# Convolving the third and fourth block of a fused conv and MLP kernel together, in bf16 quarter tiles

## The chip, the cores and the metric

The kernel runs on one core of one Trainium2 chip. The metric is the device time in microseconds (us) of one execution, as the median of several runs. The engines are TensorE (PE in the profile, with PEld for its weight loads), VectorE (DVE), ScalarE (ACT), GpSimd (POOL) and SyncE (SP, which here only starts transfers).

## The reference, cut to what matters

```python
# x: (8, 4096, 192), weight: (8, 7)
w = softmax(weight, axis=-1)                       # 8 heads, 7 taps
out[b, s, h, g] = sum_k w[h, k] * x_pad[b, s + k, h, g]    # causal depthwise conv, 24 channels a head
h = out.reshape(32768, 192) @ moe_w_in             # 192 -> 2048
g = h * sigmoid(beta * h)
y = g @ moe_w_out                                  # 2048 -> 192, float32
```

## The kernel before

The 32768 tokens are two streams `s` of 16384 tokens, which are worked on side by side. The 192 channels are cut in three groups `kk` of 64, so that 64 partitions hold one group; w_in's 2048 columns are 16 chunks `fc` of 128. The token axis is cut in steps (line 66): steps 0 and 1 have 128 tokens of each stream, step 2 has 256, steps 3 to 6 have 256 (line 68), steps 7 to 10 have 384, and the rest 512. A "block" is 128 tokens of both streams; step 0 is the first block, step 1 the second, step 2 the third and fourth. Everything here is in program order, written out by hand (`pin`).

A step has three parts. The convolution gives `xc` (bf16). The first matmul (mm1) multiplies by w_in into PSUM (`ph`), and ScalarE's Silu activation brings it to SBUF as `g`. The second matmul (mm2) multiplies by w_out, scaled by 1/beta beforehand (`scale_w_out`, line 273), into `po`; VectorE copies that out and SyncE stores it.

From step 3 on VectorE makes the convolution, tap by tap (lines 301 and 303, `conv_ops`). The first four blocks are convolved on TensorE, since VectorE has the data too late. `transpose_0` turns a block round (line 215), three matmuls of 128x128, `take_0` copies it into `xr`, channels on partitions, in fp32r: stream 0 on partitions 0 to 63, stream 1 on 64 to 127. `conv_0` makes for each tap and stream one matmul with a diagonal matrix of the tap (`diag`, line 229), 64 rows by 128 columns, so that both halves of the output hold the same data. The two streams are the two row halves of the array and run at the same time. `evac_0` (line 240) scales by the softmax's sum and writes `xcp`. As both halves hold the same, `mm1_pair` (line 325) makes two chunks at once, u with the upper and u + 8 with the lower half; it needs each chunk of w_in on one half only. From step 3 on `mm1` (line 342) makes one chunk, the two halves holding the two streams; it needs w_in on both halves. The missing halves are copied by four transfers inside SBUF (`copy_w_in`, line 116), the last entries of POOL's transfer queue.

In the text a unit (i, u) is step i and its u-th call of `mm1_pair` (8 for each of steps 0 to 2). `first_tile` (line 499) says which piece of the early work is issued behind which unit, and `first_mm2` (line 547) which mm2 of the steps before. Before the change block 1 is convolved behind (0, 1) and (0, 2); blocks 2 and 3 are turned round behind (0, 3); block 2 is convolved behind (0, 5) and (0, 6), block 3 behind (1, 0) and (1, 1); w_out's 16 chunks are scaled behind (0, 5), (0, 6) and (1, 1); mm2 of step 0 runs behind (1, 2) to (1, 7); two later blocks are turned round behind (1, 6). In step 2 mm2 has eight chunks behind each of units 1 to 4 and five or six behind the last three. `ph` has two buffers: a unit's mm1 can start when the activations of the unit two before it have ended. `vector_work` gives VectorE the taps of later steps with a budget for each unit.

Of the kernel before, what the change touches and what calls it, by code (L numbers as in the profile page):

```python
# [10 lines left out]
FP32 = mybir.dt.float32  # L11
FP32R = mybir.dt.float32r
BF16 = mybir.dt.bfloat16
AF = mybir.ActivationFunctionType
ALU = mybir.AluOpType
# [4 lines left out]
def kernel(  # L20
# [9 lines left out]
    nc = tc.nc  # L30

    B, S, D = x.shape
    H, K = weight.shape
    F = moe_w_in.shape[1]
    PAD = K - 1
# [10 lines left out]
    def pin(ins):  # L46

        return tc.keep_in_program_order(ins)
# [14 lines left out]

    steps = [(0, 128), (128, 128), (256, 256)]
    NP = len(steps)
    steps += [(t, 256) for t in range(TILE, 2 * TILE + 256, 256)]
    NQ = len(steps)
    steps += [(t, 384) for t in range(2 * TILE + 256, 4 * TILE, 384)]  # L70
# [38 lines left out]
    def half_of(s):  # L109
        return slice(64 * s, 64 * s + 64)  # L110
# [19 lines left out]
    def load_x0(b, eng):  # L130
        pin(eng.dma_start(out=x0[:, b, :, :] if b < 2 else xb0[:, b - 2, :, :],
                          in_=xs[:, 128 * b:128 * b + 128, :].rearrange("s p d -> p s d")))
# [17 lines left out]
    for f0, f1 in ((0, 256), (256, 640), (640, HF)):  # L150
        for s in range(NS):
            load_w_in(s, HF * s + f0, HF * s + f1)
        if f0 == 256:
            for b in range(2, NB):
                load_x0(b, nc.gpsimd)
    for c in range(0, NF, 4):
        pin(nc.gpsimd.dma_start(out=w_out_f[:, c:c + 4, :], in_=w_out_v[:, c:c + 4, :]))
    for s in range(NS):
# [3 lines left out]
        load_x(1, s, 2, NB, nc.gpsimd)  # L162


    xr = consts.tile([128, NK, PAD + TILE], FP32R, name="xr")
    pin(nc.vector.memset(xr[:, :, 0:PAD].bitcast(FP32), 0.0))
    ident2 = consts.tile([128, NS, Q], FP32, name="ident2")
    pin(nc.vector.tensor_tensor(out=ident2, in0=ident[:, None, 0:Q].to_broadcast([128, NS, Q]),
# [21 lines left out]
    pin(nc.tensor.matmul(tap_ps, sel.rearrange("h s g j -> h (s g j)"), taps, start=True, stop=True))  # L190
    warm(3, 128)
    pin(nc.vector.tensor_reduce(out=nmax, in_=tap_ps, axis=AX.X, op=ALU.max, negate=True))
    etap = consts.tile([128, K], FP32, name="etap")
    tsum = consts.tile([128, 1], FP32, name="tsum")
    pin(nc.scalar.activation(etap, tap_ps, AF.Exp, bias=nmax, accum_out=tsum))
    diag = consts.tile([128, K, NS, Q], FP32R, name="diag")
# [5 lines left out]
        make_diag(k)  # L202


    place = [(0, 0), (1, 0), (2, 0), (2, 128)]
    for i in range(NP):
        xc_of[i] = xc_pool.tile([128, NS, NK, steps[i][1]], BF16, name=f"xcp{i}", bufs=1)

    def transpose_0(bank, src, b):

        bf = src.dtype == BF16
        t = (bank.bitcast(BF16) if bf else bank)[:, 0:NK * 128].rearrange("p (k t) -> p k t", k=NK)
        v = src[:, b, :, :].rearrange("p s d -> p (s d)").rearrange("p (m k) -> p k m", k=NK)
        for kk in range(NK):
            pin(nc.tensor.transpose(t[:, kk, :], v[:, kk, :], ident_b if bf else ident))  # L215
        return t

    def take_0(t, b, act=False):
        dst = xr[:, :, PAD + 128 * b:PAD + 128 * b + 128]
        if act:  # L220
            pin(nc.scalar.activation(dst, t, AF.Copy))
        else:
            pin(nc.vector.tensor_copy(dst, t))
# [6 lines left out]
                    cv[s][:, 0:NK * 128], diag[half_of(s), k, :, :].rearrange("p s q -> p (s q)"),  # L230
                    xr[half_of(s), :, 128 * b + k:128 * b + k + 128], start=(k == 0), stop=(k == K - 1)))

    def evac_0(cv, b, s, eng, k0=0, k1=NK):
        i, c = place[b]
        src = cv[s][:, 128 * k0:128 * k1].rearrange("p (k t) -> p k t", t=128)
        dst = xc_of[i][:, s, k0:k1, c:c + 128]
        if eng is nc.scalar:
            pin(nc.scalar.activation(dst, src, AF.Copy, scale=rsum))
        else:
            pin(eng.tensor_scalar_mul(dst, src, rsum))  # L240
# [8 lines left out]
        make_diag(k)  # L249
    rsum = consts.tile([128, 1], FP32, name="rsum")  # L250
    pin(nc.vector.reciprocal(rsum, tsum))
    for f in range(0, HF, 512):
        for s in range(NS):
            copy_w_in(s, HF * s + f, HF * s + f + 512)
    pin(nc.scalar.activation(scrap, one, AF.Silu))
    b0 = [cv0[:, 0, :], pb[0]]
# [11 lines left out]
    pin(nc.vector.reciprocal(rbeta, beta))  # L268
    tapn = consts.tile([128, K], FP32, name="tapn")
    pin(nc.vector.tensor_scalar_mul(tapn, etap, rsum))  # L270

    def scale_w_out(c):
        pin(nc.vector.tensor_scalar_mul(w_out_s[:, c, :], w_out_f[:, c, :], rbeta[:, c:c + 1]))
# [59 lines left out]
    def mm1(i, fc):  # L333


        n = steps[i][1]
        ph = psum_h.tile([128, NS, TILE], FP32, name="ph")
        parts = [(0, 128)] if i <= NQ else [(0, 64), (64, 128)]
        for kk in range(NK):
            for m0, m1 in parts:  # L340
                for s in range(NS):
                    pin(nc.tensor.matmul(ph[m0:m1, s, 0:n],  # L342
                                         w_in_s[half_of(s), kk, 128 * fc + m0:128 * fc + m1],
                                         xc_of[i][half_of(s), kk, 0:n],
                                         start=(kk == 0), stop=(kk == NK - 1)))
        pin(nc.scalar.activation(g_at(i, fc)[:, :, 0:n], ph[:, :, 0:n], AF.Silu,  # L346
                                 scale=beta[:, fc:fc + 1]))
# [34 lines left out]
    def store(i, pr, po):  # L382
        t0 = steps[i][0]
        o_sb = osb_pool.tile([128, 2, D], FP32, name="o_sp", bufs=4)
        for q in range(2):
            take_out(o_sb[:, q, :], po[q])
        (sa, ba), (sb, bb) = pr
        if sa == sb:
            dst = os_[sa, t0 + 128 * ba:t0 + 128 * (bb + 1), :].rearrange("(b p) d -> p b d", p=128)
        else:  # L390
            dst = os_[:, t0 + 128 * ba:t0 + 128 * (ba + 1), :].rearrange("s p d -> p s d")
        pin(nc.sync.dma_start(out=dst, in_=o_sb))
# [106 lines left out]
    def first_tile(i, u):  # L499
        if (i, u) == (0, 1):  # L500
            conv_0(pb, 1, 0, 4)
        elif (i, u) == (0, 2):
            conv_0(pb, 1, 4, K)
        elif (i, u) == (0, 3):
            t23 = [transpose_0(pa[b], xb0, b) for b in range(2)]
            for b in range(2):
                take_0(t23[b], 2 + b)
            for s in range(NS):
                evac_0(pb, 1, s, nc.vector)
        elif (i, u) == (0, 5):  # L510
            conv_0(pa, 2, 0, 4)
            for c in range(4):
                scale_w_out(c)
        elif (i, u) == (0, 6):
            conv_0(pa, 2, 4, K)
            for s in range(NS):
                evac_0(pa, 2, s, nc.vector)
            for c in range(4, 8):
                scale_w_out(c)
        elif (i, u) == (1, 0):  # L520
            conv_0(pb, 3, 0, 4)
        elif (i, u) == (1, 1):
            conv_0(pb, 3, 4, K)
            for s in range(NS):
                evac_0(pb, 3, s, nc.vector)
            for c in range(8, NF):
                scale_w_out(c)
        elif (i, u) == (1, 6):
            new_xt(1)
            ts_ = [transpose_0(pb[b], xb1, b) for b in range(2)]  # L530
            for b in range(2):
                pin(nc.vector.tensor_copy(xt_of[1][:, :, LEAD + 128 * b:LEAD + 128 * b + 128], ts_[b]))
            pin(nc.vector.tensor_copy(xt_of[0][:, :, TILE + LEAD - PAD:],
                                      xr[:, :, TILE:].bitcast(FP32)))
        elif (i, u) == (1, 7):
            for s in range(NS):
                cast_x(1, s, 2, NB)
            for b in range(2, NB):
                transpose_x(1, b)
            for j in (2, 3):  # L540
                for s in range(NS):
                    load_x(j, s)
# [2 lines left out]

    prs_0 = ((0, 0), (1, 0))
    first_mm2 = {}
    for key, us, cuts in (((0, 0), [(1, u) for u in range(2, 8)], (0, 3, 6, 9, 12, 13, 16)),
# [3 lines left out]
        for (i, u), c0, c1 in zip(us, cuts, cuts[1:]):  # L552
            first_mm2[(i, u) + key] = range(c0, c1)

    for i in range(n_steps):
        plan = mm2_plan(i - 1) if NP <= i <= NQ else [[] for _ in range(NF)]
        new_g(i, 0)
        if i < NP:
            new_g(i, 1)
        if i < NP:  # L560
            for u in range(NF // 2):
                mm1_pair(i, u)
                first_tile(i, u)
                for ph in (0, 1):
                    for j in range(i):
                        for fc in first_mm2.get((i, u, j, ph), ()):
                            mm2(j, prs_0, ph, fc)
                if i == 2:
                    vector_work(i, 1300, flush=u == NF // 2 - 1)
            continue  # L570
        for u in range(NF):
            if u == NF // 2:
                new_g(i, 1)
            mm1(i, u)
            for t in plan[u]:
                mm2(i - 1, *t)
                if t[1] == 1 and t[2] == NF - 1:
                    budget -= 2 * (D + 60) / 0.96
            if i > NQ:
                mm2_quarters(NM)  # L580
            vector_work(i, 1307 * steps[i][1] // TILE, flush=u == NF - 1)
# [30 lines left out]
```

## Time and profile before

| | |
|---|---|
| median of 9 runs | 686.65 us (685.74 to 687.45) |
| the profiled execution | 686.65 us, of which the span from its first to its last instruction is 684.9 us |
| TensorE busy | 680.2 us (99%), granted clock 1.0 |
| ScalarE busy | 584.6 us (85%) |
| VectorE busy | 550.9 us (80%) |
| matmuls of `conv_0` | 56, of blocks 0 to 3 |
| start of (0, 3) | 10.58 us |
| start of step 2 | 21.17 us |
| start of the second chunk of step 3 | 31.75 us |

Times in a timeline are from the span's start. A row merges instructions of one kind that follow on each other without a gap; its first number is when the first starts, its second how long until the last ends. Matmuls are pipelined, so what a matmul costs is the distance from start to start, not its duration. A bracket names idle time before the row and what ended it.

### The profile page before, as it was taken

The numbers are of one execution on the slowest core, as the hardware profiler recorded it, in microseconds if no ns is written. First come the engines' busy times: TensorE is split into PE (matmuls) and PEld (weight loads), VectorE is DVE, ScalarE is ACT, GpSimd is POOL, SyncE is SP. The second block draws the span as 40 slices with busy tenths as digits, with TensorE's granted clock in tenths as the row PEclk, the third lists the DMA queues.
The fourth block names the chain that finished last, engine by engine and source line by source line (L and its number), as shares of the span: only waits on it lengthen the run. The fifth ranks groups of instructions, "written<-read, shape, count | busy, mean of one in ns | idle before, by whom it ended". The sixth has DMA issues, their size and how long they took to land.

```text
span 684.9 us, 27204 instructions
## 1 busy us (share of the span) xinstructions
PE 680.2 (99%) x12528; PEld 461.1 (67%) x12528; DVE 550.9 (80%) x886; ACT 584.6 (85%) x585; POOL 14.5 (2%) x26
## 2 busy tenths in 40 slices
PE   9999999999999999999999999999999999999998
PEld 7799887666666666666666666666666666666667
DVE  5999999999978889878789888889888889875112
ACT  7999999888888888888888888888888888888881
POOL 8000000000000000000000000000000000000000
PEclk9999999999999999999999999999999999999999
DMA  9653434344423344423444423344324443220213
GB/s 211 178 124 98 127 95 128 83 117 117 118 73 70 103 109 117 117 49 90 106 112 117 112 53 90 100 118 117 89 54 106 105 117 72 59 56 7 49 48 94
DMA packets 150418, 66.85 MB, mean 98 GB/s; under 512 B 113648, under 2 KB 149696, under 8 KB 150304
## 3 DMA queue, kind: packets, MB, share of 16 engines
q1 hardware_dynamic: 146992, 61.08, 35.1%
q0 software_dynamic: 3168, 3.93, 2.7%
q8 instruction: 98, 1.61, 1.0%
q14 instruction: 16, 0.13, 0.1%
q10 hardware_dynamic: 144, 0.10, 0.1%
HBM read 28.32 MB, written 25.17 MB: 78 GB/s over the span
## 4 chain that ended last, share of the span: by engine, by line
PE 98%; ACT 1%; issue 0%; DVE 0%
PE ph L342 47%; PE po L420 43%; PE po L374 4%; PE po L458 2%; PE ph L325 1%; ACT g L329 1%; PE po L229 1%; PE ph L184 0%; ACT gp L329 0%; PE ph L229 0%; PE po L215 0%; PE ph L190 0%; DVE o_sp L380 0%; PE po L263 0%
## 5 line engine op out<-in xcount | busy, mean ns | idle before, releaser
L346 ACT ACTIVATE g<-ph,beta 128x1024 bf16<-128x1024 f32 (+2 forms) x528 | 558.0, 1062 | 80.5 <-PE ph L342 62.4
L342 PE MATMUL ph<-xc,w_in_s 64*64 64x512 bf16 (+3 forms) x5952 | 617.2, 368 | 0.3 <-ACT g L329 0.3
L420 PE MATMUL po<-g,w_out_s 64*64 64x512 bf16 (+1 forms) x5568 | 580.5, 372 | 0.0
L342 PEld LDWEIGHTS <-w_in_s 64*64 64x64 bf16 (+1 forms) x5952 | 275.0, 104 | 125.7 <-issue 0.5
L420 PEld LDWEIGHTS <-w_out_s 64*64 64x64 bf16 x5568 | 289.8, 118 | 84.3
L303 DVE SCALAR_TENSOR_TENSOR acc<-xt,tapn,acc 128x512 f32<-128x512 bf16 (+2 forms) x450 | 311.1, 762 | 0.9
L437 DVE STREAM_TRANSPOSE o_sb<-po 128x512 f32<-128x512 f32 (+1 forms) x87 | 76.1, 875 | 112.4 <-PE po L420 112.3
L303 DVE SCALAR_TENSOR_TENSOR xc<-xt,tapn,acc 128x512 bf16<-128x512 bf16 (+2 forms) x90 | 64.0, 762 | 0.2
L87 DVE CAST xb<-xf 128x768 bf16<-128x768 f32 (+1 forms) x62 | 48.5, 820 | 0.0
L301 DVE TENSOR_SCALAR acc<-xt,tapn 128x512 f32<-128x512 bf16 (+2 forms) x90 | 41.0, 485 | 1.1
L374 PE MATMUL po<-w_out_s,g 64*128 64x192 bf16 x512 | 32.6, 243 | 0.0
L374 PEld LDWEIGHTS <-g 64*128 64x128 bf16 x512 | 24.8, 94 | 1.6
L380 DVE COPY o_sp<-po 128x192 f32<-128x192 f32 x28 | 9.0, 352 | 8.4 <-PE po L458 7.3
L325 PE MATMUL ph<-xcp,w_in_s 64*128 64x256 bf16 (+1 forms) x144 | 14.9, 306 | 0.2
L329 ACT ACTIVATE gp<-ph,beta 128x256 bf16<-128x256 f32 x32 | 12.6, 477 | 1.2 <-PE ph L325 0.9
L458 PEld LDWEIGHTS <-g 128*128 128x128 bf16 x128 | 10.5, 98 | 0.4 <-issue 0.4
L458 PE MATMUL po<-w_out_s,g 128*128 128x192 bf16 x128 | 10.7, 246 | 0.0
L329 ACT ACTIVATE g<-ph,beta 128x512 bf16<-128x512 f32 x16 | 9.6, 692 | 0.1
L325 PEld LDWEIGHTS <-w_in_s 64*128 64x128 bf16 x144 | 6.8, 94 | 3.5 <-issue 1.8
L229 PE MATMUL po<-xr,diag 64*128 64x384 f32 x49 | 7.9, 382 | 0.0
L374 PE MATMUL po<-w_out_s,gp 64*128 64x192 bf16 x128 | 7.6, 243 | 0.0
L374 PEld LDWEIGHTS <-gp 64*128 64x128 bf16 x128 | 5.9, 94 | 1.6
(52 smaller groups left out, 59.4 us busy)
## 6 DMA issues: line engine op xcount, KB each, us to landing
xf<-in_x_dram SPq DMA_DIRECT2D x60, 384.0 KB, 4.2
out_dram<-o_sb SPq DMA_DIRECT2D x108, 192.0 KB, 4.6
xt<-xb SPq DMA_TRANSPOSE x122, 2.8
out_dram<-o_sp SPq DMA_DIRECT2D x10, 192.0 KB, 4.2
w_out_f<-in_moe_w_out_dram POOLq DMA_DIRECT2D x4, 384.0 KB, 6.1
out_dram<-o_sb SPq DMA_DIRECT2D x8, 144.0 KB, 4.4
w_in_s<-w_in_s POOLq DMA_DIRECT2D x4, 192.0 KB, 7.4
out_dram<-o_sp SPq DMA_DIRECT2D x8, 96.0 KB, 1.9
```

The costliest lines, as they stand in the source:

```text
L87: pin((eng or nc.vector).tensor_copy(xbf_of[j][:, b0:b1, :, s, :].rearrange("p b k q -> p k b q"), xf_of[j][:, b0:b1, s, :].rearrange("p b ...
L229: pin(nc.tensor.matmul(cv[s][:, 0:NK * 128], diag[half_of(s), k, :, :].rearrange("p s q -> p (s q)"), xr[half_of(s), :, 128 * b + k:128 * ...
L301: pin(nc.vector.tensor_scalar_mul(a, src, w))
L303: pin(nc.vector.scalar_tensor_tensor(out=xc_of[i][:, k0:k1, o:o + m] if k == K - 1 else a, in0=src, scalar=w, in1=a, op0=ALU.mult, op1=ALU ...
L325: pin(nc.tensor.matmul(ph[:, h, 0:NS * n], w_in_s[half_of(h), kk, ts(fcs[h], 128)], xc_of[i][half_of(h), :, kk, :], start=(kk == 0), stop= ...
L329: pin(nc.scalar.activation(g_at(i, fcs[h])[:, :, 0:n], ph[:, h, 0:NS * n].rearrange("p (s t) -> p s t", s=NS), AF.Silu, scale=beta[:, fcs[ ...
L342: pin(nc.tensor.matmul(ph[m0:m1, s, 0:n], w_in_s[half_of(s), kk, 128 * fc + m0:128 * fc + m1], xc_of[i][half_of(s), kk, 0:n], start=(kk == ...
L346: pin(nc.scalar.activation(g_at(i, fc)[:, :, 0:n], ph[:, :, 0:n], AF.Silu, scale=beta[:, fc:fc + 1]))
L374: pin(nc.tensor.matmul(po[q][:, 0:D], g_at(i, fc)[r, s, ts(b, 128)], w_out_s[r, fc, :], start=(phase == 0 and fc == 0), stop=(phase == 1 a ...
L420: pin(nc.tensor.matmul(po_of[i, m][half_of(s), 0:n], w_out_s[half_of(r), fc, m:D:NM], g_at(i, fc)[half_of(r), s, 0:n], start=(first and fc ...
L437: pin(nc.vector.transpose(osb_of[i][:, 0:n // L, :, m], po_of[i, m][:, 0:n].rearrange("p (b l) -> p b l", l=L)))
L458: pin(nc.tensor.matmul(po[:, 0:D], g_at(i, fc)[:, s, ts(b, 128)], w_out_s[:, fc, :], start=(fc == 0), stop=(fc == NF - 1)))
```

## The change

Blocks 2 and 3 (step 2) are convolved together. Their data are taken into a bf16 tile `xrb` of their own. A bf16 diagonal `diag_b` of 64 columns holds 14 taps: seven rounded to bf16 (the fp32 tap goes through the rounding as the tile is written), seven the rest. For each of the 14 taps `conv_23` issues four matmuls of 64x64: two streams (row halves) by two blocks (column halves of the array, hence partition halves of the output). The output has a block on each half of the partitions and a stream in each of two PSUM banks.

Hence `mm1_pair` no longer serves step 2: it now takes the loop of the later steps, with 16 units of `mm1`, each with one activation. It needs both halves of w_in, and its mm2's are placed anew: four chunks behind each of units 2 to 9, two or three behind units 10 to 15. The order of the four copies of w_in is changed so that the first two complete chunks 0 to 7. The loads of blocks 2 and 3 go behind all of w_in in POOL's queue.

Block 2 is turned round and taken behind (0, 6), block 3 behind (1, 0). `conv_23` is in three pieces: 6 taps behind (1, 1), 4 behind (1, 2), 4 behind (1, 3). w_out is scaled behind (1, 1), chunks 0 to 7, and behind (1, 3) after the evacuation, chunks 8 to 15.

```diff
-    NP = len(steps)
+    ND, NP = 2, len(steps)
...
-        if f0 == 256:
-            for b in range(2, NB):
-                load_x0(b, nc.gpsimd)
+    for b in range(2, NB):
+        load_x0(b, nc.gpsimd)
...
+    xc_of[ND] = xc_pool.tile([128, NK, NS, 128], BF16, name="xcq", bufs=1)
...
+    def conv_23(cv, k0, k1):
+        for k in range(k0, k1):
+            for c in range(2):
+                for s in range(NS):
+                    t = 128 * c + k % K
+                    pin(nc.tensor.matmul(
+                        cv[s][half_of(c), 0:NK * 128], diag_b[half_of(s), k, :],
+                        xrb[half_of(s), :, t:t + 128], start=(k == 0), stop=(k == 2 * K - 1)))
...
-    for f in range(0, HF, 512):
-        for s in range(NS):
+    for s in range(NS):
+        for f in range(0, HF, 512):
             copy_w_in(s, HF * s + f, HF * s + f + 512)
...
+    tap_b = consts.tile([128, K], BF16, name="tap_b")
+    pin(nc.vector.tensor_copy(tap_b, etap))
+    pin(nc.vector.tensor_tensor(out=tap2[:, 1, :], in0=etap, in1=tap_b, op=ALU.subtract))
+    diag_b = consts.tile([128, 2 * K, Q], BF16, name="diag_b")
+    pin(nc.vector.tensor_tensor(
+        out=diag_b, in0=ident2[:, None, 0, :].to_broadcast([128, 2 * K, Q]),
+        in1=tap2.rearrange("p a k -> p (a k)")[:, :, None].to_broadcast([128, 2 * K, Q]), op=ALU.mult))
+    xrb = consts.tile([128, NK, PAD + 256], BF16, name="xrb")
+    pin(nc.vector.tensor_copy(xrb[:, :, 0:PAD], xr[:, :, 256:].bitcast(FP32)))
...
         elif (i, u) == (0, 3):
-            t23 = [transpose_0(pa[b], xb0, b) for b in range(2)]
-            for b in range(2):
-                take_0(t23[b], 2 + b)
             for s in range(NS):
                 evac_0(pb, 1, s, nc.vector)
-        elif (i, u) == (0, 5):
-            conv_0(pa, 2, 0, 4)
-            for c in range(4):
+        elif (i, u) in ((0, 6), (1, 0)):
+            b = i
+            take_0(transpose_0(pa[b], xb0, b), 2 + b)
+        elif (i, u) == (1, 1):
+            conv_23(pb, 0, 6)
+            for c in range(8):
                 scale_w_out(c)
-        elif (i, u) == (0, 6):
-            conv_0(pa, 2, 4, K)
+        elif (i, u) == (1, 2):
+            conv_23(pb, 6, 10)
+        elif (i, u) == (1, 3):
+            conv_23(pb, 10, 2 * K)
             for s in range(NS):
-                evac_0(pa, 2, s, nc.vector)
-            for c in range(4, 8):
-                scale_w_out(c)
-        elif (i, u) == (1, 0):
-            conv_0(pb, 3, 0, 4)
-        elif (i, u) == (1, 1):
-            conv_0(pb, 3, 4, K)
-            for s in range(NS):
-                evac_0(pb, 3, s, nc.vector)
+                evac_0(pb, 2, s, nc.vector)
             for c in range(8, NF):
                 scale_w_out(c)
...
-    for key, us, cuts in (((0, 0), [(1, u) for u in range(2, 8)], (0, 3, 6, 9, 12, 13, 16)),
-                          ((1, 0), [(2, 1), (2, 2)], (0, 8, 16)),
-                          ((0, 1), [(2, 3), (2, 4)], (0, 8, 16)),
-                          ((1, 1), [(2, 5), (2, 6), (2, 7)], (0, 5, 10, 16))):
+    for key, us, cuts in (((0, 0), [(1, u) for u in range(2, 8)], (0, 2, 5, 8, 10, 13, 16)),
+                          ((1, 0), [(2, u) for u in range(2, 6)], range(0, 17, 4)),
+                          ((0, 1), [(2, u) for u in range(6, 10)], range(0, 17, 4)),
+                          ((1, 1), [(2, u) for u in range(10, 16)], (0, 2, 5, 8, 10, 13, 16))):
...
-        if i < NP:
+        if i < ND:
             for u in range(NF // 2):
                 mm1_pair(i, u)
                 first_tile(i, u)
-                for ph in (0, 1):
-                    for j in range(i):
-                        for fc in first_mm2.get((i, u, j, ph), ()):
-                            mm2(j, prs_0, ph, fc)
-                if i == 2:
-                    vector_work(i, 1300, flush=u == NF // 2 - 1)
+                mm2_first(u)
             continue
         for u in range(NF):
             if u == NF // 2:
                 new_g(i, 1)
             mm1(i, u)
+            mm2_first(u)
```

More of the change, by code (lines that the diff above doesn't have):

```diff
@@ L162 @@
         load_x(1, s, 2, NB, nc.gpsimd)
-    xr = consts.tile([128, NK, PAD + TILE], FP32R, name="xr")
+    xr = consts.tile([128, NK, PAD + 256], FP32R, name="xr")
     pin(nc.vector.memset(xr[:, :, 0:PAD].bitcast(FP32), 0.0))
@@ L192 @@
     pin(nc.vector.tensor_reduce(out=nmax, in_=tap_ps, axis=AX.X, op=ALU.max, negate=True))
-    etap = consts.tile([128, K], FP32, name="etap")
+    tap2 = consts.tile([128, 2, K], FP32, name="tap2")
+    etap = tap2[:, 0, :]
     tsum = consts.tile([128, 1], FP32, name="tsum")
@@ L202 @@
         make_diag(k)
-    place = [(0, 0), (1, 0), (2, 0), (2, 128)]
-    for i in range(NP):
-        xc_of[i] = xc_pool.tile([128, NS, NK, steps[i][1]], BF16, name=f"xcp{i}", bufs=1)
+    for i in range(ND):
+        xc_of[i] = xc_pool.tile([128, NS, NK, 128], BF16, name=f"xcp{i}", bufs=1)
+    xc_of[ND] = xc_pool.tile([128, NK, NS, 128], BF16, name="xcq", bufs=1)
     def transpose_0(bank, src, b):
@@ L218, in take_0 @@
     def take_0(t, b, act=False):
-        dst = xr[:, :, PAD + 128 * b:PAD + 128 * b + 128]
+        xd, c = (xr, PAD + 128 * b) if b < 2 else (xrb, PAD + 128 * (b - 2))
+        dst = xd[:, :, c:c + 128]
         if act:
@@ L231, in conv_0, with evac_0 @@
                     xr[half_of(s), :, 128 * b + k:128 * b + k + 128], start=(k == 0), stop=(k == K - 1)))
-    def evac_0(cv, b, s, eng, k0=0, k1=NK):
-        i, c = place[b]
+    def conv_23(cv, k0, k1):
[6 more added lines that the diff above has]
+                        xrb[half_of(s), :, t:t + 128], start=(k == 0), stop=(k == 2 * K - 1)))
+    def evac_0(cv, i, s, eng, k0=0, k1=NK):
         src = cv[s][:, 128 * k0:128 * k1].rearrange("p (k t) -> p k t", t=128)
-        dst = xc_of[i][:, s, k0:k1, c:c + 128]
+        dst = xc_of[i][:, s, k0:k1, :] if i < ND else xc_of[i][:, k0:k1, s, :]
         if eng is nc.scalar:
@@ L341, in mm1 @@
                 for s in range(NS):
+                    rhs = xc_of[i][half_of(s), kk, :, :] if i == ND else xc_of[i][half_of(s), kk, 0:n]
                     pin(nc.tensor.matmul(ph[m0:m1, s, 0:n],
                                          w_in_s[half_of(s), kk, 128 * fc + m0:128 * fc + m1],
-                                         xc_of[i][half_of(s), kk, 0:n],
+                                         rhs,
                                          start=(kk == 0), stop=(kk == NK - 1)))
@@ L387, in store @@
         (sa, ba), (sb, bb) = pr
-        if sa == sb:
+        if i == ND:
+            dst = os_[:, t0 + 128 * sa:t0 + 128 * (sa + 1), :].rearrange("s p d -> p s d")
+        elif sa == sb:
             dst = os_[sa, t0 + 128 * ba:t0 + 128 * (bb + 1), :].rearrange("(b p) d -> p b d", p=128)
@@ L533, in first_tile @@
             pin(nc.vector.tensor_copy(xt_of[0][:, :, TILE + LEAD - PAD:],
-                                      xr[:, :, TILE:].bitcast(FP32)))
+                                      xrb[:, :, 256:]))
         elif (i, u) == (1, 7):
@@ L557, with mm2_first @@
         new_g(i, 0)
-        if i < NP:
+        def mm2_first(u):
+            for ph in (0, 1):
+                for j in range(i):
+                    for fc in first_mm2.get((i, u, j, ph), ()):
+                        mm2(j, prs_0, ph, fc)
+        if i < ND:
             new_g(i, 1)
-        if i < NP:
             for u in range(NF // 2):
```

## The prediction

> **What bounds the kernel now.** I read the page first, for the busy shares and the chain that ended last.
>
> ```profile
> PE 680.2 (99%) x12528; PEld 461.1 (67%) x12528; DVE 550.9 (80%) x886; ACT 584.6 (85%) x585; POOL 14.5 (2%) x26
> PE 98%; ACT 1%; issue 0%; DVE 0%
> ```
>
> TensorE sets the end almost alone. So a matmul saved anywhere, or a TensorE wait added anywhere, should pass to the end. The edit touches the first 32 us only, so next I read windows there (columns: length, then PE, PEld, DVE, ACT, POOL busy, clock, DMA).
>
> ```profile
> 10.58:31.75 21.17, 20.60 (x310) 15.52 (x309) 18.68 (x42) 20.38 (x45) 4.79 (x8) 1.00 0.84 227
> 31.75:42.27 10.52, 10.52 (x224) 10.51 (x225) 10.24 (x16) 10.47 (x17) 0.00 (x0) 1.00 0.53 143
> ```
>
> The reader is to see that up to 31.75 ScalarE is as busy as TensorE: two engines take turns in setting the pace. From the second chunk of step 3 on (31.75 us) TensorE never waits. I therefore predict when that chunk starts; all later work is unchanged and moves with it. The timeline of TensorE gives the prices:
>
> ```profile
> 14.07 1.23 PE L325 MATMUL ph<-xcp,w_in_s 64*128 64x256 bf16 x12
> 15.04 0.97 PE L229 MATMUL po<-xr,diag 64*128 64x384 f32 x8
> 15.85 0.50 PE L325 MATMUL ph<-xcp,w_in_s 64*128 64x256 bf16 x6
> 16.10 0.78 PE L229 MATMUL po<-xr,diag 64*128 64x384 f32 x6
> 16.73 0.50 PE L325 MATMUL ph<-xcp,w_in_s 64*128 64x256 bf16 x6
> 17.07 0.41 PE L374 MATMUL po<-w_out_s,gp 64*128 64x192 bf16 x6
> 17.31 0.49 PE L325 MATMUL ph<-xcp,w_in_s 64*128 64x256 bf16 x6
> 17.64 0.41 PE L374 MATMUL po<-w_out_s,gp 64*128 64x192 bf16 x6
> 18.16 0.50 PE L325 MATMUL ph<-xcp,w_in_s 64*128 64x256 bf16 x6
> 18.89 0.50 PE L325 MATMUL ph<-xcp,w_in_s 64*128 64x256 bf16 x6
> 19.62 0.50 PE L325 MATMUL ph<-xcp,w_in_s 64*128 64x256 bf16 x6
> 20.06 0.52 PE L215 MATMUL po<-ident_b,xb 128*128 128x128 bf16 x6
> 20.50 0.26 PE L374 MATMUL po<-w_out_s,gp 64*128 64x192 bf16 x2
> 31.75 0.50 PE L342 MATMUL ph<-xc,w_in_s 64*128 64x256 bf16 x6 [0.32 <-ACT g L329]
> 32.08 0.51 PE L374 MATMUL po<-w_out_s,g 64*128 64x192 bf16 x8
> 32.41 0.51 PE L342 MATMUL ph<-xc,w_in_s 64*128 64x256 bf16 x6
> ```
>
> A unit's mm1 takes 0.327 (17.31 to 17.64), three pairs of 0.109. Three mm2 chunks take 0.25 (17.07 to 17.31), 0.0825 each. Four conv_0 pairs: 15.04 to 15.85, less the 0.109 of the mm1 pair just before: 0.70, so 0.178 a pair (the three pairs, 16.10 to 16.73, agree). The six transposes start 0.056 apart; from the end of mm1 (19.62 + 0.327) to mm2 at 20.50 there are 0.55, of which 0.34 are transposes, so each of the two changes between 64x128 and 128x128 tiles costs about 0.09 to 0.1. Last, the chain of waits shows the loop with ScalarE:
>
> ```profile
> 17.27 0.85 ACT gp L329 x2
> 18.12 0.04 issue
> 18.16 0.50 PE ph L325 x6
> ```
>
> mm1 of a unit starts 0.89 after the first activation of the unit two before; activations start 0.53 after their mm1 (16.73, 17.27). So however little TensorE has to do, a unit takes at least (0.89 + 0.53) / 2 = 0.71 to 0.73: 18.16, 18.89, 19.62. In that pace TensorE has 0.72 - 0.33 = 0.39 a unit for other work; what it doesn't use there is lost, and what exceeds it delays.
>
> **The change, on TensorE alone.** Removed: 14 conv_0 pairs, 14 x 0.178 = 2.49. Added: 14 rounds of four 64x64 matmuls of 384 columns. No such round is in this stage, but step 7 has the same shape:
>
> ```profile
> 75.77 0.49 PE L374 MATMUL po<-w_out_s,g 64*128 64x192 bf16 x7
> 76.19 0.68 PE L342 MATMUL ph<-xc,w_in_s 64*64 64x384 bf16 x12
> 76.70 0.49 PE L420 MATMUL po<-g,w_out_s 64*64 64x384 bf16 x4
> ```
>
> Twelve matmuls in 0.51: 0.17 a round of four, so 14 x 0.17 = 2.38. The first starts 0.173 after the last mm2 (whose 0.243 ended at 76.26), where 0.083 is usual: a change to 64x64 tiles costs 0.09. Three pieces change there and back, 6 x 0.09 = 0.54. The bf16 rounds thus cost 2.92 against 2.49. Two groups of three transposes instead of one of six add two more changes, 0.19. TensorE's work grows by 0.63.
>
> [...]
>
> Step 2: 16 units of 0.327 are as much as 8 of 0.648 (six matmuls of 512, from 0.216 a pair); with 48 mm2 chunks, 5.23 + 3.96 = 9.19 both before and after. ScalarE still has 16 activations of 128x512.
>
> **Where the work stands.** Total TensorE work from (0, 3), at 10.58 in both, to 31.75: 13 mm1 4.25, transposes 0.52 + 0.52, conv 2.49, mm2 of step 0 1.32, step 2 9.19, one chunk of step 3 0.66: 18.95, so 2.22 of the 21.17 us are idle. After, 19.58 of work. Its idle I get by stepping through the units with the loop above (start of mm1, before and forecast):
>
> (0,4) 11.47, 11.15; (0,5) 12.02, 12.02; (0,6) 13.19, 12.74; (0,7) 14.07, 13.45; (1,0) 14.80, 14.17; (1,1) 15.85, 14.88; (1,2) 16.73, 16.46; (1,3) 17.31, 17.81; (1,4) 18.16, 19.24; (1,5) 18.89, 19.82; (1,6) 19.62, 20.83; (1,7) 20.60, 21.93; (2,0) 21.17, 22.51.
>
> Up to (1, 1) the forecast is a unit's worth ahead, since the conv work is gone: it runs at ScalarE's pace, and TensorE idles 1.6 over six units, two of which have transposes to fill the gap. At (1, 1) six rounds come at once: 0.33 + 6 x 0.1625 + 0.19 and about 0.07 of waiting for block 3, taken by VectorE 0.4 after its transposes. That is 1.58 against a pace of 0.72. (1, 2) and (1, 3) have 4 rounds each and two or three mm2 chunks: 1.35 and 1.43. The lead is spent and 1.1 lost by (1, 4).
>
> VectorE: the casts and `diag_b` go behind `tapn`, where it sat idle 2.17 before L223. 896 elements cost about 1.1, by the 0.29 of the 128x128 sum on line 168 plus 768 elements at 0.96 a ns; with the small ones 1.7, done at 11.0. Evacuation of block 1 follows at once, earlier than before (12.41). Without that cover it would be 1.7 late, still ahead of (1, 0). Scaling chunks 8 to 15 is now queued behind the evacuation, which waits for the last round (about 19.06): two evacuations of 0.53, then 0.23 a chunk. Chunk 8 is there at 20.5, chunk 9 at 20.75, but mm2 wants them behind (1, 5) at 20.15: TensorE waits 0.4. VectorE's taps for step 3 then start about 1.6 later (23.6 for 22.07) and end at 31.3, before step 3 wants them at 33.0.
>
> Step 2: its first two units have no mm2; (2,1) and (2,2) wait for ScalarE 0.50 and 0.24. The last six have less mm2 (0.49 to 0.58 of work against 0.57 for an activation) and lose 0.55. The old ends of this step, 0.3 at (2,1) and 0.5 at 31.75, go. The second chunk of step 3 comes at 33.68 for 31.75: +0.63 of work, +1.30 of idle, **+1.93**.
>
> Transfers: POOL issues as many. xb0's two loads go behind two loads of w_in of 0.62 each, so they land about 1.2 later, near 10.9; wanted at 13. The copies of w_in land at 21.06, 21.76, 22.04 and 22.52 (L116 issues at 12.9 to 16.2, 6.3 to 8.2 to landing); chunks 0, 4, 8 and 12 of step 2 want them at 22.5, 25.3, 27.9 and 30.5. They cost nothing, but they would hold (2, 0) at 21.1, were it early. SP is passed by nothing.
>
> **Sum.** The profiled execution took 686.65, 1.75 of it outside the span of 684.9, and that is the median too. 686.65 + 1.93 = **688.6 us**. About 0.2%, 1.37 us, is what a measurement of this kernel can tell from no change.
>
> **Rivals.** [...]
> (C) Not slower: TensorE's new idle is no more than the old. The mechanism is the ScalarE pace: if the early lead carries through (mm2 and rounds in (1,1) to (1,3) fitting without the waits at w_out and at step 2's ends), only the work counts: 686.65 + 0.63 = 687.3. It decides where idle between 10.58 and the second chunk of step 3 is under 2.22 + 1.37 - 0.63 = 2.96 instead of 3.5. For it: step 2 is divided finer. Against: 1.6 is lost before the first round.
> (D) Faster. From (1, 1), which ScalarE forbids before 14.88, 16.9 of work remain: 31.8 at best, no gain. Even with the rounds' changes of tiling free it is 31.2, a gain of 0.5. It would need rounds at half the price of the row, giving about 685.
>
> **How the numbers follow.** The likeliest, 0.67, is 688.1 to 689.2; B 0.19; C 0.10; D 0.04. Slower by over 0.2% 0.86, within 0.10, faster 0.04. For 8 in 10 the range leaves out D and half of C, and about a quarter of B: 687.4 to 690.0.
>
> **What would show it.** In the profile after: rounds on the new conv line 0.16 to 0.17 apart (0.21: serial weights); 0.09 at each change; (1, 1) at 14.9 and (1, 4) at 19.2; mm2 waiting for line `scale_w_out` behind (1, 5); step 2 at 22.5; step 3's second chunk at 33.7, and nothing changed after it. If (1, 4) starts before 18.5, or VectorE isn't what mm2 waits for, my stepping is wrong.

## The result, and the profile after

The changed kernel takes 688.89 us as the median of 9 runs (688.53 to 689.56), against 686.74 for the kernel before (29 runs). The ratio is 1.0033, with a 95% interval of 1.0025 to 1.0041: slower by 2.15 us, where 1.93 had been forecast.

The page of the kernel after: its busy row, its chain, and two of its groups of instructions:

```profile
PE 682.2 (99%) x12604; PEld 463.7 (67%) x12604; DVE 551.1 (80%) x888; ACT 585.2 (85%) x585; POOL 14.5 (2%) x26
...
PE 98%; ACT 1%; DVE 0%; issue 0%
...
L364 PE MATMUL ph<-xcq,w_in_s 64*128 64x256 bf16 x96 | 8.1, 269 | 0.4 <-ACT gp L350 0.4
...
L396 PE MATMUL po<-w_out_s,gp 64*128 64x192 bf16 x128 | 9.0, 243 | 0.2 <-DVE w_out_s L294 0.2
```

There are 76 matmuls more (28 for the rounds, 48 for step 2). Two waits of TensorE are new among the groups: for ScalarE at step 2, for w_out's scaled chunks behind (1, 5). The timeline of TensorE after: (0, 3), and from (1, 1) on:

```profile
11.39 1.10 PE L346 MATMUL ph<-xcp,w_in_s 64*128 64x256 bf16 x12
...
15.76 0.50 PE L346 MATMUL ph<-xcp,w_in_s 64*128 64x256 bf16 x6
16.19 1.25 PE L242 MATMUL po<-xrb,diag_b 64*64 64x384 bf16 x24
17.37 0.50 PE L346 MATMUL ph<-xcp,w_in_s 64*128 64x256 bf16 x6
17.80 0.85 PE L242 MATMUL po<-xrb,diag_b 64*64 64x384 bf16 x16
18.58 0.34 PE L396 MATMUL po<-w_out_s,gp 64*128 64x192 bf16 x4
18.76 0.49 PE L346 MATMUL ph<-xcp,w_in_s 64*128 64x256 bf16 x6
19.18 0.85 PE L242 MATMUL po<-xrb,diag_b 64*64 64x384 bf16 x16
19.96 0.42 PE L396 MATMUL po<-w_out_s,gp 64*128 64x192 bf16 x6
20.22 0.49 PE L346 MATMUL ph<-xcp,w_in_s 64*128 64x256 bf16 x6
...
21.50 0.49 PE L396 MATMUL po<-w_out_s,gp 64*128 64x192 bf16 x4 [0.21 <-DVE w_out_s L294]
...
23.53 0.49 PE L364 MATMUL ph<-xcq,w_in_s 64*128 64x256 bf16 x6
...
34.75 0.51 PE L364 MATMUL ph<-xc,w_in_s 64*128 64x256 bf16 x6
```

Six rounds fill 16.19 to 17.37. A unit that holds them takes 1.61 (15.76 to 17.37), the next two 1.39 and 1.46, where ScalarE's pace is 0.72. ScalarE's own timeline shows the other side: it starves three times in these units.

```profile
17.91 0.84 ACT L350 ACTIVATE gp<-ph,beta 128x256 bf16<-128x256 f32 x2 [0.75 <-PE ph L346]
19.29 0.84 ACT L350 ACTIVATE gp<-ph,beta 128x256 bf16<-128x256 f32 x2 [0.54 <-PE ph L346]
20.75 2.07 ACT L350 ACTIVATE gp<-ph,beta 128x256 bf16<-128x256 f32 x5 [0.62 <-PE ph L346]
```

Earlier it is TensorE that waits, before (0, 5), (0, 6) and (1, 0), as more rows of its timeline show; with no conv work there, it has nothing to do at ScalarE's pace:

```profile
12.84 0.50 PE L346 MATMUL ph<-xcp,w_in_s 64*128 64x256 bf16 x6 [0.35 <-ACT gp L350]
13.57 0.50 PE L346 MATMUL ph<-xcp,w_in_s 64*128 64x256 bf16 x6 [0.22 <-ACT gp L350]
...
15.03 0.50 PE L346 MATMUL ph<-xcp,w_in_s 64*128 64x256 bf16 x6 [0.23 <-ACT gp L350]
```

The two profiled executions differ by 3.0 us in span (684.9, 687.9), more than the medians. The difference lies ahead of the stretch that I predicted: (0, 3) starts at 11.39 here and at 10.58 before, which is how these two executions happened to start (the last section has the spread). So I count from (0, 3). To the second chunk of step 3 it is 23.36 us after (34.75 - 11.39) and 21.17 before: +2.19. Behind that chunk both have 653.1 us to the end of the span (687.9 - 34.75, 684.9 - 31.75). All of the change lies between these two points. The medians say the same without a profile: they differ by 2.15, so over many executions there is no sign that the change moved the start.

### The profile page after: what moved, and what is told of

The parts are those of the page before. It is cut to its first block, busy times and chain, and to the rows that moved or that the text cites. A ratio compares the mean times of both kernels' runs of the same rounds, so it can differ in the third digit from the quotient of the medians.

```text
span 687.9 us, 27357 instructions
## 1 busy us (share of the span) xinstructions
PE 682.2 (99%) x12604; PEld 463.7 (67%) x12604; DVE 551.1 (80%) x888; ACT 585.2 (85%) x585; POOL 14.5 (2%) x26
## 3 DMA queue, kind: packets, MB, share of 16 engines
q8 instruction: 98, 1.61, 1.0%
## 4 chain that ended last, share of the span: by engine, by line
PE 98%; ACT 1%; DVE 0%; issue 0%
PE ph L364 48%; PE po L444 43%; PE po L396 4%; PE po L482 2%; ACT gp L350 1%; PE ph L184 0%; PE ph L346 0%; PE po L242 0%; PE ph L231 0%; PE po L216 0%; DVE xcq L252 0%; ACT g L368 0%; PE ph L190 0%; DVE o_sp L402 0%; DVE w_out_s L294 0%
## 5 line engine op out<-in xcount | busy, mean ns | idle before, releaser
L368 ACT ACTIVATE g<-ph,beta 128x1024 bf16<-128x1024 f32 (+2 forms) x544 | 568.3, 1050 | 80.5 <-PE ph L364 62.4
L364 PEld LDWEIGHTS <-w_in_s 64*64 64x64 bf16 (+1 forms) x6048 | 279.8, 104 | 126.2 <-issue 1.0
L396 PE MATMUL po<-w_out_s,gp 64*128 64x192 bf16 x128 | 9.0, 243 | 0.2 <-DVE w_out_s L294 0.2
L346 PE MATMUL ph<-xcp,w_in_s 64*128 64x256 bf16 x96 | 8.1, 277 | 0.9 <-ACT gp L350 0.8
L364 PE MATMUL ph<-xcq,w_in_s 64*128 64x256 bf16 x96 | 8.1, 269 | 0.4 <-ACT gp L350 0.4
L346 PEld LDWEIGHTS <-w_in_s 64*128 64x128 bf16 x96 | 4.5, 97 | 2.7 <-issue 2.1
L231 PE MATMUL po<-xr,diag 64*128 64x384 f32 x21 | 4.4, 421 | 0.0
```

The source lines that it names most:

```text
L346: pin(nc.tensor.matmul(ph[:, h, 0:NS * n], w_in_s[half_of(h), kk, ts(fcs[h], 128)], xc_of[i][half_of(h), :, kk, :], start=(kk == 0), stop= ...
L364: pin(nc.tensor.matmul(ph[m0:m1, s, 0:n], w_in_s[half_of(s), kk, 128 * fc + m0:128 * fc + m1], rhs, start=(kk == 0), stop=(kk == NK - 1)))
L396: pin(nc.tensor.matmul(po[q][:, 0:D], g_at(i, fc)[r, s, ts(b, 128)], w_out_s[r, fc, :], start=(phase == 0 and fc == 0), stop=(phase == 1 a ...
```

## The experiments

Two numbers are read from each: the median, and the stretch from (0, 3) to the second chunk of step 3 in its profile ("the stretch"), which leaves out most of how the start went; the two profiles with the earliest starts have 0.09 more between (0, 3) and (1, 1). The stretch is 21.17 in the kernel before, 23.36 in the changed one.

**Step 2 alone.** The kernel before, with the fp32r convolution evacuated by halves into the new layout, and step 2 as in the change:

```diff
-        dst = xc_of[i][:, s, k0:k1, c:c + 128]
+        r = slice(0, 128) if i < ND else half_of(b - 2)
+        dst = xc_of[i][:, s, k0:k1, :] if i < ND else xc_of[i][r, k0:k1, s, :]
...
-                          ((1, 0), [(2, 1), (2, 2)], (0, 8, 16)),
+                          ((1, 0), [(2, u) for u in range(2, 6)], range(0, 17, 4)),
```

> The kernel before with its fp32r convolutions where they were, and only step 2 as in the change: 16 units of mm1 on a block for each half of the partitions, mm2 spread over them, w_in's copies in the new order. Theory of the forecast (work on TensorE plus idle at ScalarE's pace): the work is the same 9.19, but step 2 with the first chunk of step 3 takes about 11.1 instead of 10.58 us, so +0.5 us, 687.2. Rival (the whole loss is the price of the 64x64 rounds and their changes of tiling): none is left, so 686.7, no change. A copy of w_in that lands after 21.1 could hold unit (2, 0) for some tenths.

Measured: 687.87 us (21 runs), ratio 1.0014, interval 1.0007 to 1.0020. The stretch is 22.49, 1.32 more than before where 0.5 was expected. TensorE's timeline shows what came on top:

```profile
20.89 0.41 PE L380 MATMUL po<-w_out_s,gp 64*128 64x192 bf16 x6
21.14 0.27 PE L348 MATMUL ph<-xcq,w_in_s 64*128 64x256 bf16 x1
21.97 0.82 PE L348 MATMUL ph<-xcq,w_in_s 64*128 64x256 bf16 x11 [0.56 <-DMA w_in_s<-w_in_s]
23.25 0.28 PE L348 MATMUL ph<-xcq,w_in_s 64*128 64x256 bf16 x2 [0.45 <-ACT g L352]
```

The first matmul of step 2 runs at 21.14; the second needs the half of w_in that is copied, and that copy lands at 21.93. Before, only step 3 needed the copies; the new step 2 needs them a whole step earlier. It holds the weight load for 0.81, and both the rival (no change) and my 0.5 fall.

**Step 2 alone, without need of the copies.** To divide the two, step 2 takes columns that were loaded on each half directly:

```diff
-                                         w_in_s[half_of(s), kk, 128 * fc + m0:128 * fc + m1],
+                    f0 = 128 * (fc % 8 + 8 * s) if i == ND else 128 * fc
...
+                                         w_in_s[half_of(s), kk, f0 + m0:f0 + m1],
```

> The kernel before with step 2 alone as in the change, needing no copy (columns of w_in that were loaded on that half directly, wrong for one of the two blocks). Theory: the wait of 0.81 for the copy behind (2, 0) is gone and only the finer division of step 2 is left, 0.45 to 0.65 over the kernel before: from (0, 3) to the second chunk of step 3 21.65 to 21.8 us, 687.2 to 687.4. Rival (the division costs nothing, the copies all): 686.75.

Measured: 687.39 us (11 runs), ratio 1.0007, interval 0.9998 to 1.0016; the stretch is 21.83 (32.61 - 10.78), +0.66. The time alone would not settle it, but the stretch does: the wait is gone, and 0.66 is left for the division of step 2. So the wait of 0.81 had cost 0.66 of the stretch (22.49 - 21.83). From (2, 0) on, 11.23 here and 11.22 in the changed kernel stand against 10.58. A part of the loss is at the head, where the first two units have no mm2. In TensorE's timeline the second waits for ScalarE:

```profile
21.38 0.49 PE L349 MATMUL ph<-xcq,w_in_s 64*128 64x256 bf16 x6
22.23 1.08 PE L349 MATMUL ph<-xcq,w_in_s 64*128 64x256 bf16 x12 [0.36 <-ACT gp L334]
```

**The rounds earlier.** The changed kernel with its rounds where the fp32r convolution had been:

```diff
+        elif (i, u) == (0, 5):
+            conv_23(pa, 0, 6)
...
+        elif (i, u) == (0, 6):
+            conv_23(pa, 6, 10)
...
+        elif (i, u) == (0, 7):
+            conv_23(pa, 10, 2 * K)
```

> The changed kernel with its rounds placed where blocks 2 and 3 were convolved before: both blocks turned round and taken behind (0, 3), 6, 4 and 4 rounds behind (0, 5), (0, 6), (0, 7), their loads back in the middle of w_in's, w_out scaled behind (0, 5), (0, 6) and (1, 1). Theory of the forecast: the idle from (0, 3) to (1, 0) is filled, but (1, 0) to (1, 5) then run at ScalarE's pace; one group of transposes less. About 0.7 us less than the changed kernel, 688.2, still 1.3 to 1.5 over the kernel before. Rival (rounds and changes of tiling are the whole loss): 0.2 us less (one group of transposes), 688.7. Rival (the late place is the whole loss): back to 686.8.

Measured: 688.56 us (10 runs), ratio 1.0023, interval 1.0013 to 1.0032. The stretch is 22.71 (34.05 - 11.34): 0.65 less than in the changed kernel, as my theory had it (0.7), and 1.54 over the kernel before (1.3 to 1.5):

```profile
11.34 0.52 PE L347 MATMUL ph<-xcp,w_in_s 64*128 64x256 bf16 x6
...
19.65 0.50 PE L347 MATMUL ph<-xcp,w_in_s 64*128 64x256 bf16 x6
...
22.83 0.49 PE L365 MATMUL ph<-xcq,w_in_s 64*128 64x256 bf16 x6
...
34.05 0.51 PE L365 MATMUL ph<-xc,w_in_s 64*128 64x256 bf16 x6
```

From (0, 3) to (1, 4), where the rounds moved, it is 8.31 (19.65 - 11.34) against 8.83 (20.22 - 11.39): 0.52 less. The other 0.13 come between (1, 4) and (2, 0), where the wait for w_out is gone too. The median falls by 0.33 only; its interval overlaps that of the changed kernel (1.0025 to 1.0041), so the time can't choose between 0.2 and 0.7. The stretch leaves both rivals out: the late place is a part of the loss, not the whole.

**Half of the rounds.** The seven rounds of the remainders are left out:

```diff
-            conv_23(pb, 0, 6)
+            conv_23(pb, 0, 3)
...
-            conv_23(pb, 6, 10)
+            conv_23(pb, 3, 5)
...
-            conv_23(pb, 10, 2 * K)
+            conv_23(pb, 5, K)
```

> The changed kernel without the seven matmul rounds of the taps' remainders: 3, 2 and 2 rounds behind (1, 1), (1, 2), (1, 3) instead of 6, 4 and 4, so the convolution of blocks 2 and 3 has taps rounded to bf16. Theory of the forecast: every round lies in a unit above ScalarE's pace, so 7 x 0.163 = 1.15 us less than the changed kernel, 687.75. [...] Rival (the rounds lie in ScalarE's shadow): under 0.3 less.

Measured: the stretch is 22.20 (33.42 - 11.22), 1.16 less than in the changed kernel; expected were 1.15. So a round is worth its 0.163 or so on the path. But the median is 688.30 us (13 runs), only 0.59 less.

**One round, with and without the copies.** The gap between stretch and median pointed to a floor: a time before which step 2 can't go on, however early the first part ends. First, all rounds but one were left out:

```diff
-            conv_23(pb, 0, 6)
+            conv_23(pb, 0, 1)
...
-            conv_23(pb, 6, 10)
...
-            conv_23(pb, 10, 2 * K)
```

> The changed kernel with one round instead of 14 (the convolution of blocks 2 and 3 is left out but for the first tap). The run before last showed w_in's copies landing at 21.9 us and holding step 2. Theory (work and pace, with the copies as a floor): step 2 gets to about 20.2 to 20.5 but its first unit waits for the copy until 21.9 or so; from (0, 3) to the second chunk of step 3 about 22.4 us, against 23.36 in the changed kernel and 21.17 before: about 687.8, so the new step 2 alone keeps the kernel over 1 us slower. Rival (no floor): 21.2 to 21.4, about 686.8. Rival (the rounds make no difference): 688.9.

Measured: 687.75 us (11 runs), as the floor predicts, but with a stretch of 21.38, as the rival predicts. In this execution step 2 began at 21.50 after a late start, and the first copy had landed at 21.45, so it had no copy to wait for. The same kernel without need of the copies, and the one with seven rounds likewise:

> The kernel with one round, where step 2 also takes for each half of the partitions columns of w_in that were loaded there directly (wrong columns for one of the two blocks), so that it needs none of the four copies. Theory (the copies' landing is a floor for step 2, which a late start of the array hides): 0.6 to 1.0 us less than with one round and the copies (687.75), 686.8 to 687.1. Rival (no floor; that kernel's executions happened to start late): no change, 687.75.

> The kernel with seven of the 14 rounds, needing no copy in step 2 (columns as in the run before). Theory (floor by the copies): 687.65 to 687.9, so that seven rounds are worth their 7 x 0.163 = 1.15 of the changed kernel's time. Rival (no floor): 688.3 as with the copies.

With one round: 687.11 us (11 runs), 0.64 less; the lowest execution goes from 687.56 to 686.61. The profiled one was the longest (687.82), and its stretch of 21.72 holds a wait for a load that the profile with the copies doesn't have:

```profile
20.45 0.49 PE L216 MATMUL po<-ident_b,xb 128*128 128x128 bf16 x6 [0.46 <-DMA xb<-in_x_dram]
```

With seven rounds: 688.29 us, the same median as with the copies (688.30), a miss of the floor theory as I had put it in numbers; both profiled executions started late and have the same stretch (22.20, 22.21). The single times say more than the median. With the copies 12 of 13 lie from 688.16 to 688.70. Without them five lie from 687.22 to 687.73 and six from 688.29 to 688.61. An early start gains about 1 us only where no copy is needed. The runs with and without the copies were made apart, so a rival is that early starts were rare in the first. Against it stand the executions of the kernel before made beside them: under 687.1, that is early, lie 29 of 42 beside the seven rounds with copies, 16 of 23 beside the one round with copies, and 22 of 28 beside the two runs without. This fits a floor: where the first part is fast, the copies, which land at a time of their own, hold step 2. No profile shows an early start with one or seven rounds and the copies, so for these kernels the floor is inferred from the times. In profiles it is seen in the run of step 2 alone and, small, in that of the one piece below.

**The changed kernel without need of the copies.**

> The changed kernel, needing no copy in step 2 (columns as in the runs before). Theory: the copies land before its late step 2 wants them, so no change, 688.7 to 689.0. Rival (the copies hold it in the executions that start early): 0.3 or more less.

Measured: 688.45 us (6 runs, 688.05 to 688.96), ratio 1.0030, interval 1.0018 to 1.0041. The median is 0.44 less than the changed kernel's, on the rival's side, but against 1.0033 (1.0025 to 1.0041) that decides nothing. In the changed kernel's profile the first copy lands at 22.43 us and step 2 starts at 23.53. This run's profile has an early start, (0, 3) at 9.96: its step 2 starts at 22.18, and the first copy, which it doesn't need, lands at 21.77. So an early start leaves a margin of some tenths or none.

**The scaling first.** Chunks 8 to 15 of w_out are scaled behind (1, 2), ahead of the evacuation:

```diff
         elif (i, u) == (1, 2):
             conv_23(pb, 6, 10)
+            for c in range(8, NF):
+                scale_w_out(c)
...
-            for c in range(8, NF):
-                scale_w_out(c)
```

> The changed kernel with w_out's chunks 8 to 15 scaled behind (1, 2), ahead of the evacuation of the rounds on VectorE, instead of behind it. Theory of the forecast: TensorE no longer waits for the scaled chunks behind (1, 5); as ScalarE's pace holds (1, 6) anyway, 0.2 us less than the changed kernel, 688.7, and the row of the wait is gone. Rival (the wait costs its whole 0.43): 688.45. Rival (chunks 12 to 15 of w_out land late and now delay the evacuation): no gain or some tenths slower.

Measured: 688.68 us (9 runs), ratio 1.0030 (1.0020 to 1.0039), too near to the changed kernel for the time to tell. The stretch is 23.18, 0.18 less, and its timeline has the second row without the wait; ScalarE's pace takes over at (1, 6):

```profile
20.17 0.49 PE L346 MATMUL ph<-xcp,w_in_s 64*128 64x256 bf16 x6
20.50 0.33 PE L396 MATMUL po<-w_out_s,gp 64*128 64x192 bf16 x4
21.02 0.50 PE L346 MATMUL ph<-xcp,w_in_s 64*128 64x256 bf16 x6 [0.19 <-ACT gp L350]
```

**All rounds in one piece.**

```diff
-            conv_23(pb, 0, 6)
+            conv_23(pb, 0, 2 * K)
...
-            conv_23(pb, 6, 10)
...
-            conv_23(pb, 10, 2 * K)
```

> The changed kernel with all 14 rounds in one piece behind (1, 1) instead of 6, 4 and 4. Theory of the forecast: four changes of tiling of 0.09 fewer, of which some is lost again to ScalarE's pace in the units behind: 0.2 to 0.3 us less than the changed kernel, 688.6 to 688.7. [...] Rival (bunching costs more than the changes): slower than 688.9.

Measured: 688.85 us (7 runs), ratio 1.0028 (1.0017 to 1.0039); the stretch is 23.21, 0.15 less. The time tells nothing, but the stretch fits the forecast: this execution started early, and beside the changed kernel without need of the copies, which started as early and has 23.45, it is 0.24 less (0.2 to 0.3 were expected). Four changes of tiling at 0.09 are 0.36; what is missing goes to the pace of the units behind. The rows show the piece, and the head of step 2:

```profile
14.96 0.50 PE L346 MATMUL ph<-xcp,w_in_s 64*128 64x256 bf16 x6
15.40 2.56 PE L242 MATMUL po<-xrb,diag_b 64*64 64x384 bf16 x56
17.89 0.50 PE L346 MATMUL ph<-xcp,w_in_s 64*128 64x256 bf16 x6
...
22.50 0.63 PE L364 MATMUL ph<-xcq,w_in_s 64*128 64x256 bf16 x6
```

From 15.40 to 17.89 are 2.49 us for 14 rounds and the change back: 0.09 and 14 x 0.165, with the first round 0.02 longer than the others, and 0.07 from the first matmul of a round to its last (16.190 to 16.266 in the profile after). At 22.50 six matmuls take 0.63 where 0.49 is usual: the first copy lands at 22.59, and the second matmul starts at 22.63. It costs nothing here, since the next unit waits for ScalarE anyway and starts 0.85 later, as in the changed kernel.

**A version that beats both.** If idle at the pace is what costs, the kernel before has some to win too: its conv_0 pairs come 3 or 4 to a unit (0.86 to 1.04 us with mm1, above 0.72), while other units have none. Its pairs need no change of tiling: they have the 64x128 tiles of mm1, and mm1 with three of them takes 0.88 (15.85 to 16.73 before), where their prices add up to 0.86. So they can be dealt out one by one:

```diff
+        elif (i, u) == (0, 5):
+            conv_0(pa, 2, 0, 2)
+        elif (i, u) == (0, 6):
+            conv_0(pa, 2, 2, 4)
+        elif (i, u) == (0, 7):
+            conv_0(pa, 2, 4, K)
...
+    for iu, n in zip([(1, u) for u in range(2, 8)] + [(2, u) for u in range(8)],
+                     (0, 2, 4, 4, 1, 2, 5, 5, 6, 6, 6, 7, 5, 11)):
```

> The kernel before (fp32r, step 2 in 8 units of mm1_pair), its early work only dealt out anew so that a unit of steps 0 and 1 stays near ScalarE's pace of 0.72: conv_0 pairs 4, 1, 2 behind (0, 1), (0, 2), (0, 4) for block 1, 2, 2, 3 behind (0, 5) to (0, 7) for block 2, 2, 2, 2, 1 behind (1, 0) to (1, 3) for block 3; mm2 chunks 2, 4, 4, 1, 2 behind (1, 3) to (1, 7) and 5, 5, 6, 6, 6, 7, 5, 11 behind step 2's units. Theory (the work of TensorE is the same, its idle at ScalarE's pace is what can be won): step 2 at about 20.0 to 20.4 instead of 21.2, the second chunk of step 3 some 1.0 to 1.4 us earlier, 685.3 to 685.7. Rival (the early stage's length is set by transfers or by VectorE's taps for step 3, not by pace): no gain, 686.5 to 686.9.

Measured: 686.00 us (11 runs, 684.92 to 686.21) against 686.78 beside it: ratio 0.9984, interval 0.9975 to 0.9993. The gain is clear, but at 0.78 it is smaller than forecast (685.3 to 685.7). The stretch is 20.11, 1.06 less than before (1.0 to 1.4 were forecast): 0.64 of it up to (1, 1), 0.31 behind (2, 0), where mm2 is dealt out anew too. Counted from (0, 2), ahead of the first moved pair, it is 20.77 (30.53 - 9.76) against 22.05. The windows of the stretch, first in the changed kernel, with the columns as in the prediction:

```profile
11.39:34.75 23.36, 21.84 (x387) 17.01 (x386) 18.22 (x42) 21.07 (x45) 4.63 (x7) 1.00 0.78 199
```

and in this version:

```profile
10.42:30.53 20.11, 20.11 (x315) 15.78 (x313) 18.42 (x41) 19.99 (x45) 4.95 (x8) 1.00 0.86 234
```

Before, TensorE was busy for 20.60 of 21.17 and ScalarE for 20.38; after, for 21.84 and 21.07 of 23.36; here TensorE for all of it and ScalarE for all but 0.12. As ScalarE's work is given, little is left to win in this stage by order alone.

## Why the prediction was right

By stretches, before, forecast and measured: (0, 3) to (1, 1) 5.27, 4.30, 4.37; (1, 1) to (1, 4) 2.31, 4.36, 4.46; (1, 4) to (2, 0) 3.01, 3.27, 3.31; (2, 0) to the second chunk of step 3 10.58, 11.17, 11.22. The lead gained and lost again, and the 0.6 of step 2, are all there. The sum is +2.19 for +1.93.

*The rounds.* Forecast 0.1625 to 0.17; in the trace 0.162 to 0.168, and 0.188 to 0.193 for the first. The weight loads last 104 ns, four of them 0.42 us, so they overlap (four start at 16.548, 16.551, 16.593 and 16.624). No run shows a round of 0.21 (serial weights), nor the terms that would make the rounds dearer than in step 7 (the B of the chances, most of which is in the range up to 690.0). The runs show 0.162 to 0.168 a round, and 1.16 for seven rounds in the half-rounds run. (Step 7, from which the price was read, is a step of 384 tokens, as the prediction has it; by lines 68 to 70 steps 3 to 5 have 256 and steps 6 and 7 have 384, not 3 to 6 and 7 to 10.)

*The changes of tiling.* Forecast 0.09 each. Into the rounds 0.199 from start to start, where 0.109 is usual; out of them 0.255, where 0.163 is: 0.09 both times. For the transposes the prediction's own sum, (0.55 - 0.34) / 2, is 0.11 and not 0.09 to 0.1. That made no difference: units (0, 6) and (1, 0) take ScalarE's 0.73 with their transposes (13.57 to 14.30, 15.03 to 15.76).

*The idle at ScalarE's pace.* Forecast as the main term, and the runs bear it out from both sides: moving the rounds into idle units wins 0.52, and dealing the old work out at the pace wins 1.06 on the kernel before. Rival C is out: by the forecast's prices idle is 3.78 (23.36 - 19.58), not under 2.96.

*The wait for w_out.* Forecast 0.4, with VectorE behind the evacuation. The wait was there and as long: mm2 could have started at 21.12 (20.79 + 0.33) and starts at 21.50. But taking it away won 0.18 only, since ScalarE's pace would have held (1, 6) anyway. As a price, 0.4 would be too much. Ahead of it, on VectorE, `diag_b` took 1.09 where 1.1 was forecast; the 0.96 elements a ns in that forecast are the pace of the taps before (line 303: 616 ns for 384, 1419 for 1152).

*Step 2.* Forecast 0.59 more from (2, 0) on (11.17 against 10.58), measured 0.64 here and 0.65 in the run without copies.

*The copies.* "They cost nothing" was a weak step, and that it came true is in part luck. I took one landing, 21.06, for a fixed time. The first copy lands at 22.43 in the profile after and anywhere from 21.31 to 22.86 in those of the other runs, where step 2 was to start at 22.5. They stay hidden in the profiled execution, since the work is late as well; the run of step 2 alone shows what they can cost, 0.66. Had the first stage been as quick as hoped for, the copies would have taken a part of the gain.

*What is left.* The stretch exceeds the forecast by 0.26: 0.07 and 0.10 in the first two parts, about 0.05 in each of the others. No single cause was found for it. Nor do the runs divide all of the 2.19: 0.65 is step 2, 0.52 the late place of the rounds, 0.13 to 0.18 the wait for w_out. For the other 0.9 or so, that 14 bf16 rounds with their changes of tiling cost more than 14 fp32r pairs (2.92 against 2.49 by the forecast's prices) and that units above and below the pace lose the rest is argued from the rows; no run took it apart.

## What to carry to other kernels

Where two engines take turns, work out the pace of the loop between them and lay each unit's work against it: what a unit doesn't use is lost, and what exceeds it delays, so work bunched in few units costs even when the total stays, and dealing it out won 1.06 us here. Matmuls of another tiling cost 0.09 us at each change here, which asks for few large pieces, while the pace asks for many small ones; work in the tiling of its neighbours has no such conflict. And when a change makes a stage want a transfer earlier, look at when it lands, even where the first profile shows it hidden.

## What the runs showed of the hardware

The start of an execution differs from run to run. In the timelines of before and after, the conv_0 pairs of the first block are 0.32 apart from the second on; before, the step falls to 0.18 from the sixth pair on; after, it is still 0.32 at the seventh. First the kernel before, then the changed one:

```profile
6.61 0.47 PE L229 MATMUL ph<-xr,diag 64*128 64x384 f32 x1
...
6.92 0.34 PE L229 MATMUL ph<-xr,diag 64*128 64x384 f32 x1
...
7.10 0.34 PE L229 MATMUL ph<-xr,diag 64*128 64x384 f32 x1
...
8.08 0.95 PE L325 MATMUL ph<-xcp,w_in_s 64*128 64x256 bf16 x12
```

```profile
6.69 0.52 PE L231 MATMUL ph<-xr,diag 64*128 64x384 f32 x1
...
7.01 0.52 PE L231 MATMUL ph<-xr,diag 64*128 64x384 f32 x1
...
7.33 0.52 PE L231 MATMUL ph<-xr,diag 64*128 64x384 f32 x1
```

In the runs of the one piece and of the changed kernel without copies the pairs are 0.18 apart from the second on, and step 0 starts at 7.2 us; elsewhere at 8.0 to 8.3 or at 8.7 to 8.8. The granted clock reads 1.00 all the same (4.5 to 9.5 us, before and after). The point at which the step falls to 0.18 lies anywhere from before 5.4 to after 7.3 us. In the changed kernel and its variants with the same first stage (0, 3) starts anywhere from 9.96 to 11.39 us. That is more than most effects of this study, and it is why a stretch inside one profile told more than a median here. A part of an early start is lost again: in the run of the one piece (0, 2) waits for a load of w_in.

```profile
9.74 0.39 PE L346 MATMUL ph<-xcp,w_in_s 64*128 64x256 bf16 x4 [0.68 <-DMA w_in_s<-in_moe_w_in_dram]
```

What sets the point at which the step falls to 0.18 was not tested.
